# Batch 0's head: Q fetched by head halves, the first columns of w_in in four row chunks, one log and one scaling moved up, four fillers fewer

## The chip, the cores and the metric

The kernel runs on one core of a Trainium2 chip. The metric is device microseconds of that core; lower is better. A time covers a whole execution. The span, which the profile covers, is 1.7 to 1.9 us shorter in the runs of the kernel before: it runs from the first recorded instruction to the end of the last.

In the views, PE is TensorE's matmuls, PEld its weight loads, DVE is VectorE, ACT ScalarE, POOL GpSimd and SP SyncE; L674 is a line of the kernel. A landing is the moment at which the last byte of a transfer has arrived.

## The reference, cut to what matters

```python
def _attn_ref(q, k, v, g_norm):              # q, k, v: 8 batches, 8 heads, 576 rows, 64 columns
    kv = np.einsum('bhsd,bhse->bhde', k, v)
    out = np.einsum('bhsd,bhde->bhse', q, kv)
    rms = np.sqrt(np.mean(out * out, axis=-1, keepdims=True) + 1e-06)
    return out / rms * g_norm

def _moe_ref(x, w_in, w_out):                # 4608 x 512, 512 x 2048, 2048 x 512
    h = x @ w_in
    g = np.where(h > 0.0, h, np.exp(np.minimum(h, 0.0)) - 1.0)
    return g @ w_out
```

Linear attention without a softmax, a normalisation per head, then two dense products with an ELU between them. The two dense products are nearly all of the work, and TensorE (PE in the profile) does them.

## The kernel before: the parts that the change and the argument touch

Batch 0 has a head of its own. "Head" below means this first stretch of some 20 us, not an attention head. The order of the transfers (all on the GpSimd queue, except Q's two on SyncE's):

```python
fetch_q(0)                                   # two transfers of 512 KB: heads 0,2,4,6 then 1,3,5,7
packed_kv(0)
for c in range(4):                           # K and V of batch 0 in four pieces of 144 KB each
    fetch_packed_kv("k", 0, slice(c, c + 1))
    ...
    fetch_packed_kv("v", 0, slice(c, c + 1))
edges = (0, 512, 768, 1280, 1664, 2048)
for lo, hi in zip(edges, edges[1:]):         # w_in by columns, all 512 rows at a time
    load_w_in(slice(lo, hi))
load_w_out(0, 4)
fetch_packed_q(1)
load_w_out(4, 8)
packed_kv(1)
for name in "kv":
    fetch_packed_kv(name, 1, slice(0, 2))    # K and V of batch 1, first half
load_w_out(8, 10)
for name in "kv":
    fetch_packed_kv(name, 1, slice(2, 4))    # second half
```

The compute of the head goes by four chunks c of 128 rows of x transposed. Each is a K/V product, a score product, a square, a mean over the head's columns (a matmul with a matrix of 1/64), Ln, Exp with scale -0.5 (this is 1/rms), and a scaling on VectorE (DVE). Then come the first 24 products with w_in, six blocks of 128 columns, f, for four chunks, c. `idle(ps, n)` issues n filler matmuls on zeros.

```python
def square_first(c): nc.scalar.activation(sq0[c], se0[c], AF.Square)
def mean_first(c):   nc.tensor.matmul(mean0[c], lhsT=means, rhs=sq0[c], start=True, stop=True)
def log_first(c):    nc.scalar.activation(r0[c], mean0[c], AF.Ln, bias=eps_col)
def exp_first(c):    nc.scalar.activation(r0[c], r0[c], AF.Exp, scale=-0.5)
def scale_first(c):  nc.vector.scalar_tensor_tensor(out=x0[:, c, :], in0=se0[c], scalar=g_col,
                                                    in1=r0[c], op0=ALU.mult, op1=ALU.mult)
def first(fs, cs):
    for c in cs:
        for f in fs:
            nc.tensor.matmul(products[f], lhsT=w_in_sb[:, c, f * P : f * P + P],
                             rhs=x0[:, c, :], start=(c == 0), stop=(c == KC - 1))
...
se0[3] = bank(3)
se_first(3)
square_first(3)
exp_first(2)
idle(bank(0), 2)
scale_first(1)
scale_first(2)
...
first((0, 1, 2, 3), (0,))
mean0[3] = bank(2)
mean_first(3)
log_first(3)
exp_first(3)
scale_first(3)
products[5] = bank(1)
first((0, 1, 2, 3), (1, 2))
first((4,), (0, 1, 2))
first((0, 1, 2, 3), (3,))
first((5,), (0, 1, 2))
first((4, 5), (3,))
```

## Time and profile before

| | before |
|---|---|
| time, median of the first three runs | 284.17 us (284.15 to 284.39) |
| PE busy, share of the span | 98% |
| first product with w_in | 14.76 us |
| last Exp of the head starts | 16.77 us |
| next product stream after the head starts | 20.27 us |
| V of batch 1, second half: lands / the K/V product that needs it starts | 37.85 / 38.85 us |

The page's first part (busy microseconds, share of the span, instructions of each engine) and its fourth (the chain of work that ended last) of the kernel before:

```profile
PE 277.2 (98%) x2146; PEld 129.7 (46%) x2146; DVE 159.3 (56%) x231; ACT 154.5 (55%) x222; POOL 54.7 (19%) x96
...
PE 95%; DMA 2%; DVE 1%; SPq 0%; issue 0%; ACT 0%
```

PE is the bottleneck and waits for almost nothing. So only a stretch where PE has no useful work can give time, and that is the head.

The timeline of the kernel before, around the head and around batch 1. The columns are start, microseconds, engine, line, operation, output and inputs; brackets hold the idle time just before and what ended it:

```profile
14.76 0.33 PEld L674 LDWEIGHTS <-w_in_sb 128*128 128x128 bf16 x3 [0.39 <-DMA w_in_sb<-in_moe_w_in_dram]
14.76 0.60 PE L674 MATMUL h_ps<-xT,w_in_sb 128*128 128x512 bf16 x2
...
16.77 0.63 ACT L662 ACTIVATE r<-r 128x512 f32<-128x512 f32 x1
...
17.43 0.75 DVE L665 SCALAR_TENSOR_TENSOR xT<-bank,g_col,r 128x512 bf16<-128x512 f32 x1 [0.67 <-ACT r L662]
...
20.27 1.03 PE L465 MATMUL h_ps<-xT,w_in_sb 128*128 128x512 bf16 x4
...
38.85 0.48 PE L174 MATMUL at<-v_pk,k_pk 64*64 64x64 bf16 x36
```

The first product waits for w_in, which lands at 14.72. The K/V product at 38.85 has no bracket (one is printed for an idle time of 0.15 us and more): its V had landed a whole microsecond earlier.

```profile
q0 software_dynamic: 3334, 2.94, 90.9%
```

The transfers move about 205 GB/s from some 6 us to beyond 40 us without a pause. Apart from Q's two and the small g_norm, every transfer of the first 40 us stands in one line behind the others.

### The profile page before, as it was taken

Reading aid. Unit: us, or ns where it says so; the run is one execution under the profiler, and the core shown is the slowest. Engines: PE = TensorE matmul, PEld = TensorE weight load, DVE = VectorE, ACT = ScalarE, POOL = GpSimd, SP = SyncE. Lnnn points to the kernel's source line nnn. Section 1 sums busy time; section 2 is a strip of 40 time slices with the busy share of each in tenths; the row PEclk is TensorE's granted clock in tenths of the full one; section 3 lists DMA queues with packets and bytes.
Section 4 is the critical chain, followed back from the end, with each engine's and each line's share of the span. In section 5 each row is a group of like instructions: output and inputs, shape, how many; then the busy total and the mean of one; then the engine's idle time right before and its main releaser. Section 6 shows DMA issues by size and latency. Waiting matters only on the chain.

```text
span 282.7 us, 5187 instructions
## 1 busy us (share of the span) xinstructions
PE 277.2 (98%) x2146; PEld 129.7 (46%) x2146; DVE 159.3 (56%) x231; ACT 154.5 (55%) x222; POOL 54.7 (19%) x96
## 2 busy tenths in 40 slices
PE   7999999999999999999999999999999999999994
PEld 3444454445444444444444444444444444444443
DVE  2359443878388646944694468445854585444400
ACT  2779546667487438533863377237923792333311
POOL 7834422261421331005200421012000000000000
PEclk9999999999999999999999999999999999999999
DMA  7999999797993696358935794455233122010122
GB/s 194 203 204 202 208 200 185 220 152 129 187 190 62 154 166 148 74 148 124 196 75 145 93 216 84 116 115 150 55 97 73 78 53 95 0 77 0 74 74 77
DMA packets 56523, 35.99 MB, mean 127 GB/s; under 512 B 32820, under 2 KB 54068, under 8 KB 56500
## 3 DMA queue, kind: packets, MB, share of 16 engines
q0 software_dynamic: 20752, 17.30, 39.9%
q1 hardware_dynamic: 35348, 17.83, 23.7%
q10 hardware_dynamic: 400, 0.52, 0.6%
q8 instruction: 17, 0.28, 0.4%
q14 instruction: 6, 0.05, 0.0%
HBM read 36.70 MB, written 9.44 MB: 163 GB/s over the span
## 4 chain that ended last, share of the span: by engine, by line
PE 95%; DMA 2%; DVE 1%; SPq 0%; issue 0%; ACT 0%
PE h_ps L465 41%; PE o_ps L512 39%; PE o_ps L917 5%; DMA st_q<-in_q_dram 2%; PE at L174 2%; PE bank L674 1%; PE at L465 1%; PE at L201 1%; PE h_ps L674 1%; PE bank L596 1%; PE bank L644 1%; PE se_ps L201 1%; PE kv_ps L174 0%; PE at L185 0%; PE se_ps L413 0%; PE bank L656 0%
## 5 line engine op out<-in xcount | busy, mean ns | idle before, releaser
L465 PE MATMUL h_ps<-xT,w_in_sb 128*128 128x512 bf16 x536 | 125.7, 379 | 0.0
L512 PE MATMUL o_ps<-w_out_sb,gT 128*128 128x512 bf16 x512 | 120.5, 379 | 0.0
L477 ACT ACTIVATE elu_e<-h_ps 128x1024 bf16<-128x1024 f32 (+1 forms) x71 | 70.0, 995 | 79.9 <-PE h_ps L465 78.3
L465 PEld LDWEIGHTS <-w_in_sb 128*128 128x128 bf16 x552 | 52.5, 98 | 63.2 <-DVE xT L333 1.7
L512 PEld LDWEIGHTS <-gT 128*128 128x128 bf16 x512 | 49.4, 98 | 58.4
L488 DVE TENSOR_SCALAR elu_e<-elu_e 128x1024 bf16<-128x1024 bf16 (+1 forms) x75 | 32.3, 431 | 72.9 <-ACT elu_e L477 72.9
L496 DVE TENSOR_TENSOR gT<-elu_e,h_ps 128x1024 bf16<-128x1024 bf16 (+1 forms) x51 | 60.1, 1179 | 5.7 <-DVE elu_e L488 0.5
L525 ACT COPY o_sb<-o_ps 128x512 f32<-128x512 f32 x32 | 18.6, 586 | 15.6 <-PE o_ps L512 15.6
L218 DVE TENSOR_REDUCE ss<-sq 128x16 f32<-128x1024 bf16 x16 | 19.4, 1219 | 10.8 <-ACT sq L213 10.1
L483 ACT ACTIVATE elu_h<-h_ps 128x1024 bf16<-128x1024 f32 (+1 forms) x20 | 19.5, 990 | 0.0
L150 POOL COPY q_bf<-q_pk 128x512 bf16<-128x512 bf16 x24 | 14.6, 638 | 21.6 <-DMA q_pk<-in_q_dram 21.6
L496 DVE TENSOR_TENSOR gT<-elu_e,elu_h 128x1024 bf16<-128x1024 bf16 x20 | 13.8, 692 | 2.9 <-ACT elu_h L483 1.5
L917 PE MATMUL o_ps<-w_out_sb,gT 128*128 128x512 bf16 (+1 forms) x80 | 14.1, 337 | 0.0
L125 POOL COPY gate<-qT 1x1 bf16<-1x1 bf16 x6 | 1.1, 182 | 63.7 <-DMA qT<-q_bf 63.7
L104 POOL DMA_DIRECT2D q_pk<-in_q_dram x14 | 10.6, 762 | 2.8 <-issue 1.1
L229 DVE TENSOR_TENSOR xs<-at,ss 128x512 bf16<-128x512 f32 x16 | 10.3, 682 | 1.2 <-ACT ss L225 1.2
L917 PEld LDWEIGHTS <-gT 128*128 128x128 bf16 x80 | 7.7, 98 | 6.4 <-DVE gT L496 0.4
L213 ACT ACTIVATE sq<-at 128x1024 bf16<-128x1024 f32 x9 | 9.4, 1043 | 1.6 <-PE at L201 1.0
L118 POOL DMA_DIRECT2D k_pk<-in_k_dram x12 | 8.3, 691 | 4.5 <-DMA w_in_sb<-in_moe_w_in_dram 2.9
L596 PE MATMUL bank<-zeros 128*128 128x512 bf16 x20 | 7.8, 515 | 1.2 <-DVE zeros L573 1.2
L118 POOL DMA_DIRECT2D v_pk<-in_v_dram x12 | 8.2, 684 | 3.7 <-DMA w_out_sb<-in_moe_w_out_dram 1.8
L925 ACT COPY o_last<-o_ps 128x512 f32<-128x512 f32 (+1 forms) x5 | 2.5, 501 | 10.8 <-PE o_ps L917 10.8
(79 smaller groups left out, 139.4 us busy)
## 6 DMA issues: line engine op xcount, KB each, us to landing
out_dram<-o_sb SPq DMA_DIRECT2D x16, 512.0 KB, 3.0
q_pk<-in_q_dram POOLq DMA_DIRECT2D x14, 256.0 KB, 4.8
k_pk<-in_k_dram POOLq DMA_DIRECT2D x6, 576.0 KB, 8.3
v_pk<-in_v_dram POOLq DMA_DIRECT2D x6, 576.0 KB, 10.8
st_q<-in_q_dram SPq DMA_DIRECT2D x2, 512.0 KB, 5.1
w_in_sb<-in_moe_w_in_dram POOLq DMA_DIRECT2D x2, 512.0 KB, 8.8
w_out_sb<-in_moe_w_out_dram POOLq DMA_DIRECT2D x2, 512.0 KB, 15.2
w_out_sb<-in_moe_w_out_dram POOLq DMA_DIRECT2D x4, 256.0 KB, 11.8
```

Source lines behind the costliest of these rows:

```text
L118: nc.gpsimd.dma_start(out=raw[name, b].rearrange("p h j d -> p h (j d)")[:, hs], in_=in_[:, hs])
L150: eng.tensor_copy(out=out_, in_=in_)
L218: nc.vector.reduce_sum(out=ss, in_=sq.rearrange("p c (h e) -> p (c h) e", h=H), axis=AX.X)
L465: nc.tensor.matmul(h_ps[a][:, cs], lhsT=w_in_sb[:, c, f * P : f * P + P], rhs=x(c, cs), start=(c == 0), stop=(c == KC - 1),)
L477: nc.scalar.activation(e[:, lo:hi, :], ps, AF.Exp)
L483: nc.scalar.activation(h[:, lo:hi, :], ps, AF.Relu)
L488: nc.vector.tensor_scalar(out=e[:, lo:hi, :], in0=e[:, lo:hi, :], scalar1=1.0, scalar2=1.0, op0=ALU.min, op1=ALU.subtract,)
L496: nc.vector.tensor_tensor(out=gT[T][:, 2 * i + lo : 2 * i + hi, :], in0=e[:, lo:hi, :], in1=h, op=ALU.add if relu else ALU.max,)
L512: nc.tensor.matmul(o_ps[T, j], lhsT=gT[T][:, f, j * P : j * P + P], rhs=w_out_sb[:, f, :], start=(f == 0), stop=(f == FC - 1),)
L525: nc.scalar.copy(o_sb[T][:, j % 2, :], o_ps.pop((T, j)))
L596: nc.tensor.matmul(ps, lhsT=zeros[:, 0:P], rhs=zeros, start=True, stop=True)
L917: nc.tensor.matmul(ps, lhsT=gT[B][:, f, j * P : j * P + P], rhs=w_out_sb[:, f, cols], start=(f == 0), stop=(f == FC - 1),)
```

## The change

Its intent: w_in's first 512 columns should arrive by row chunks, so that the products of chunk 0 can start before all 512 KB are there. Q should come by head halves, so that the two head pairs that chunks 0 and 1 need arrive with the first transfer. Chunk 1's mean and log move ahead of chunk 2's score product and square, and chunk 0's scaling moves up, so that ScalarE's chain of Ln and Exp runs closer together. The 24 products are reordered, and net four filler matmuls go. Cut to its core:

```diff
-    fetch_q(0)
+    for u in range(2):                       # heads 0-3, then heads 4-7
+        nc.sync.dma_start(out=q_raw0[:, u]..., in_=q[0, 4 * u : 4 * u + 4, 0:G, :]...)
@@
-    edges = (0, 512, 768, 1280, 1664, 2048)
+    for c in range(KC):
+        load_w_in(slice(0, 512), slice(c, c + 1))
+        if c == 1:
+            load_w_in(slice(512, 768))
+    edges = (768, 1024, 1280, 1664, 2048)
@@
-    turn_first(qt_ps, (0, 1))
+    turn_first(qt_ps, (0, 2))
@@
     kv_first(0)
-    idle(idle_ps, 1)
+    turn_last(7, 1)
     se0[0] = bank(6)
     se_first(0)
     square_first(0)
@@
     log_first(0)
-    se0[1] = bank(7)
-    se_first(1)
-    square_first(1)
-    exp_first(0)
     g_ps = bank(1)
     nc.tensor.matmul(g_ps[:, 0:1], ...)      # g_norm, turned into a column
+    idle(idle_ps, 1)
+    se0[1] = bank(7)
+    se_first(1)
+    square_first(1)
+    exp_first(0)
@@
     kv_first(2)
-    idle(idle_ps, 2)
+    mean0[1] = bank(0)
+    mean_first(1)
+    log_first(1)
     se0[2] = bank(1)                         # then, as before, score product, square, exp_first(1)
     ...
+    scale_first(0)                           # taken out further down, with mean and log of chunk 1
@@
     se_first(3)
     square_first(3)
     exp_first(2)
-    idle(bank(0), 2)
     ...
-    first((0, 1, 2, 3), (1, 2))
-    first((4,), (0, 1, 2))
-    first((0, 1, 2, 3), (3,))
-    first((5,), (0, 1, 2))
-    first((4, 5), (3,))
+    first((0, 1, 2, 3), (1,))
+    first((4,), (0, 1))
+    first((0, 1, 2, 3, 4), (2, 3))
+    first((5,), range(KC))
```

The bytes moved are the same; there are four more transfers of w_in.

More of the change, by code (lines that the diff above doesn't have):

```diff
@@ L133, in unpack_q, with load_w_in @@
             copy_on(eng, bf["q", b][:, j], t[:, :, j])
-    def load_w_in(cols):
+    def load_w_in(cols, cs=slice(0, KC)):
         nc.gpsimd.dma_start(
-            out=w_in_sb[:, :, cols], in_=moe_w_in.rearrange("(c p) f -> p c f", p=P)[:, :, cols]
+            out=w_in_sb[:, cs, cols],
+            in_=moe_w_in.rearrange("(c p) f -> p c f", p=P)[:, cs, cols],
         )
@@ L549 @@
     V, A, Q = nc.vector, nc.scalar, nc.gpsimd
-    fetch_q(0)
-    q_raw0 = raw.pop(("q", 0))
+    q_raw0 = stage_tile("q")[:, 0:2048].rearrange("p (u x) -> p u x", u=2)
+    for u in range(2):
+        nc.sync.dma_start(
+            out=q_raw0[:, u].rearrange("p (h x) -> p h x", h=4),
+            in_=q[0, 4 * u : 4 * u + 4, 0:G, :].rearrange("h (p j) d -> p h (j d)", j=J),
+        )
     packed_kv(0)
@@ L603 @@
     idle(idle_ps, 9)
-    q_st = q_raw0.rearrange("p (q h j d) -> p q j h d", q=4, h=2, j=J)
+    q_st = q_raw0.rearrange("p u (l s j d) -> p u s j l d", l=2, s=2, j=J)
     q_two = attp.tile([P, NPAIR, J, 2, D], BF16, name="q_two", tag="q_two", bufs=1)
@@ L608, in cast_first @@
     def cast_first(pair, eng):
-        copy_on(eng, q_two[:, pair], q_st[:, pair])
+        copy_on(eng, q_two[:, pair], q_st[:, pair % 2, pair // 2])
     def turn_first(ps, pairs):
@@ L619 @@
     cast_first(0, V)
-    cast_first(1, A)
+    cast_first(2, A)
     qt_ps = turned(3)
-    turn_first(qt_ps, (0, 1))
-    nc.vector.tensor_copy(out=qT0[:, 0:2], in_=qt_ps)
+    turn_first(qt_ps, (0, 2))
+    nc.vector.tensor_copy(
+        out=qT0.rearrange("p (s u) t -> p u s t", u=2)[:, 0], in_=qt_ps
+    )
     idle(idle_ps, 4)
-    cast_first(2, V)
+    cast_first(1, V)
     cast_first(3, A)
@@ L680, in first, with turn_last @@
                 )
-    qt_ps = turned(7)
-    turn_first(qt_ps, (2,))
-    nc.scalar.copy(qT0[:, 2, :], qt_ps[:, 0, :])
+    def turn_last(n, pair):
+        qt_ps = turned(n)
+        turn_first(qt_ps, (pair,))
+        nc.vector.tensor_copy(out=qT0[:, pair, :], in_=qt_ps[:, 0, :])
     kv_first(0)
-    idle(idle_ps, 1)
+    turn_last(7, 1)
     se0[0] = bank(6)
@@ L689 @@
     square_first(0)
-    qt_ps = turned(0)
-    turn_first(qt_ps, (3,))
-    nc.vector.tensor_copy(out=qT0[:, 3, :], in_=qt_ps[:, 0, :])
-    idle_ps = bank(3)
+    turn_last(0, 3)
     kv_first(1)
@@ L709 @@
     )
+    idle_ps = bank(3)
+    idle(idle_ps, 1)
[3 more added lines that the diff above has]
+    exp_first(0)
     nc.vector.tensor_copy(out=g_col, in_=g_ps[:, 0:1])
+    idle(idle_ps, 1)
     kv_first(2)
-    idle(idle_ps, 2)
+    mean0[1] = bank(0)
+    mean_first(1)
+    log_first(1)
     se0[2] = bank(1)
@@ L715 @@
     square_first(2)
-    mean0[1] = bank(0)
-    mean_first(1)
-    log_first(1)
     exp_first(1)
+    scale_first(0)
     idle(idle_ps, 1)
     kv_first(3)
-    scale_first(0)
-    idle(idle_ps, 1)
     mean0[2] = bank(2)
@@ L734 @@
     pair = ps_head.tile([P, 2, G], FP32, name="h_ps", tag="kv")
-    products = {0: pair[:, 0, :], 1: pair[:, 1, :], 2: bank(6), 3: bank(7), 4: bank(0)}
+    products = {0: pair[:, 0, :], 1: pair[:, 1, :], 2: bank(6), 3: bank(0), 4: bank(7)}
     first((0, 1, 2, 3), (0,))
```

## The prediction

> **What bounds the kernel.** TensorE is busy 98% of the span (engine table) and the chain of waits is 95% PE. From 20.3 us on, the matmul starts show no gap over 0.31 us: 0.216 us per 512-column product, nothing else waited for. So only the head, before the first dense product stream, can give time. In the head: Q's two transfers land at 4.98 and 7.28 us (issue start plus time to landing), the K/V pieces one after another from 7.09 to 12.17, w_in's first 512 columns at 14.72. First product at 14.76, its weight load having waited 0.4 us for that transfer (waits). The head's 24 products plus one mean take 5.4 us at 0.216 each; the next product starts at 20.27: nearly dense from 14.8. So before is held by the landing of w_in's first piece, and just behind it by ScalarE: its last Exp ends at 17.40, the last scaling on VectorE at 18.18 (timeline).
>
> **What the change does.** The DMA queue is saturated here: 512 KB in 14.72-12.17 = 2.55 us, about 0.64 us per 128 KB row chunk. Estimated landings: rows 0 at 12.8, rows 1 at 13.5, columns 512-767 at 14.9, rows 2 and 3 at 15.5 and 16.1 (perhaps 1 us later: columns 512-767 took 2.3 us before, a straggler). Same bytes, four more transfers; their issues (0.55 to 0.75 us) stay ahead of the data. The weights no longer gate the first product.
>
> Head halves: pairs 0 and 2, all that chunks 0 and 1 need, come with the first Q transfer. Chunk 0's K/V product then waits only for V at 7.81 instead of running behind pair transposes at 8.11: start 7.87, first square 9.20 (was 9.44). A ScalarE copy (0.59) moves to VectorE. Net four filler matmuls (0.22 each) go.
>
> By the durations of before (square to Exp start 0.48, Exp to log 0.54, log to square 0.57, log to own Exp 0.72): logs at 10.26, 12.23, 13.86, 15.48; last Exp ends 16.83, last scaling 17.62. The last score product comes before the first product: first product about 14.1 (was 14.76). Then c=0 to 14.95, mean of chunk 3 about 15.06 (a small stall), c=1 from 15.3, c=2 from 16.6, c=3 from 17.68 just after the last scaling, f=5 last. Next product near 19.62 instead of 20.27: 0.65 us, all on the critical path.
>
> **Does it survive?** Later DMA landings stay where they are, bandwidth-bound: columns 768 on near 18.4 against use at 19.5; V of batch 1 (second half) lands 37.85, used at 38.85 before, so at 38.2 now. Slack about 0.4: a gain over 1.0 would be cut there. ScalarE, full from 20 to 28, starts its ELU work 0.8 us earlier too.
>
> **Prediction:** 283.5 us, range 283.1 to 284.0.
>
> **Right or wrong shows in:** first product near 14.1, not waiting for DMA; ScalarE's last head Exp ending near 16.8; the last scaling near 17.6; the first product after the head near 19.6; no new DMA wait on PE from 20 to 55; gap list after that unchanged.
>
> **What would make it wrong:** the small w_in pieces landing over 1 us late, moving the wait to columns 512-767 or rows 2 and 3; VectorE, in order, delaying a K/V copy behind a transposed-Q copy (0.42 each), so chunk 1's square starts late; [...] this trace shows fillers 0.43 us apart until 7.1 us and 0.22 after[...].

The gain is the 0.65 us from 20.27 to 19.62, off the 284.17 us before, so 283.5. Two statements have their figures in the traces: ScalarE was busy for 8.00 of the 8 us from 20 to 28 (before), and VectorE's order did cost chunk 1 a little (after: its K/V product ended at 10.06, its copy started at 10.15, behind a transposed-Q copy that ended at 10.12).

## More of the kernel before

The windows view of the kernel before (stretch, its length, busy time and instructions of PE, PEld, DVE, ACT and POOL, then the granted PE clock, the DMA share and the GB/s), and from the DMA view of its first 20 us the GpSimd queue's line (packets, MB, share):

```profile
11.00:13.00 2.00, 2.00 (x28) 0.87 (x28) 0.44 (x2) 1.63 (x4) 2.00 (x4) 1.00 1.23 205
...
16.00:20.00 4.00, 4.00 (x20) 1.76 (x18) 1.50 (x2) 2.36 (x4) 1.24 (x2) 1.00 1.29 204
```

## The result, and the profile after

| | before, same rounds | after |
|---|---|---|
| median | 284.21 us (284.15 to 284.39, 4 runs) | 284.54 us (284.26 to 285.21, 4 runs) |
| ratio after to before | | 1.0014, 95% interval 0.9996 to 1.0032 |

Ratios here are the mean time of one kernel's fast runs over the mean of the other's of the same rounds, so not quite the ratio of the medians. The result is "the same" at 2%, and no gain can be seen. The predicted 283.5 us was wrong, and so was its range: the median lies outside, above.

The same parts of the page after (source lines have moved: 465 is now 466, 174 is 175, 512 is 513, 674 is 685):

```profile
PE 274.2 (97%) x2111; PEld 130.0 (46%) x2142; DVE 159.8 (57%) x232; ACT 153.9 (54%) x221; POOL 56.7 (20%) x100
...
PE 84%; DMA 11%; POOL 2%; issue 1%; ACT 0%; POOLq 0%
```

PE's busy time fell (some matmul records are missing from a trace, so the 3 us are not to be taken at their word), but the span did not: both traced executions span 282.7 us. New in the chain is DMA, with 11%. The timeline after, at the same places:

```profile
8.08 0.47 PE L175 MATMUL kv_ps<-v_pk,k_pk 64*64 64x64 bf16 x18 [0.88 <-DMA v_pk<-in_v_dram]
...
10.95 0.40 PE L655 MATMUL bank<-qT,kv 64*64 64x512 bf16 x2 [0.25 <-DVE g_col L722]
...
14.33 0.61 PE L685 MATMUL h_ps<-xT,w_in_sb 128*128 128x512 bf16 x2
...
16.46 0.63 ACT L673 ACTIVATE r<-r 128x512 f32<-128x512 f32 x1
...
17.12 0.75 DVE L676 SCALAR_TENSOR_TENSOR xT<-bank,g_col,r 128x512 bf16<-128x512 f32 x1 [0.55 <-ACT r L673]
...
19.87 1.03 PE L466 MATMUL h_ps<-xT,w_in_sb 128*128 128x512 bf16 x4
...
38.68 0.48 PE L175 MATMUL at<-v_pk,k_pk 64*64 64x64 bf16 x36 [0.16 <-DMA v_pk<-in_v_dram]
```

The head did what it should. The first product no longer waits for w_in and starts at 14.33 instead of 14.76; the stream after the head starts at 19.87 instead of 20.27, 0.40 earlier. But at 38.68 there is a bracket that before did not have: the K/V product of batch 1 now waits for V. The chain of waits after shows the same, in order of time (start, microseconds, what):

```profile
14.20 11.90 DMA w_out_sb<-in_moe_w_out_dram
26.10 0.29 issue
26.39 12.15 DMA v_pk<-in_v_dram
38.54 0.14 issue
38.68 0.48 PE at L175 x36
```

V now lands at 26.39 + 12.15 = 38.54 us, 0.69 later than before's 37.85. The chain runs back through the queue: V's transfer is issued only when an earlier one has landed (w_out's at 26.10; GpSimd had waited 1.82 us for it, and as long in the kernel before, where V was issued at 25.92), so a delay of the early transfers is handed on. The same windows and the queue's line after:

```profile
11.00:13.00 2.00, 1.97 (x25) 0.81 (x25) 0.74 (x2) 1.72 (x4) 1.78 (x4) 1.00 1.20 179
...
16.00:20.00 4.00, 4.00 (x20) 1.83 (x19) 1.72 (x3) 2.50 (x5) 2.36 (x5) 1.00 1.39 198
```

```profile
q0 software_dynamic: 3769, 2.84, 93.5%
```

By 20 us the queue has moved 2.84 MB where it had moved 2.94, in more packets. 0.10 MB at 204 GB/s are 0.5 us: an estimate from these two traces that accounts for most of the 0.69. The other traces agree on the bytes: 2.94 to 2.96 MB in the four with before's transfers of w_in, 2.81 to 2.91 in the twelve with split ones.

To see what becomes of the 0.40 us, I matched each PE weight load after the head with the same one of the before trace, and took the difference of their start times. A step in this offset is a place where one kernel waits and the other does not.

| place in the before trace | 20.3 us | 39.5 | 58 | 90 | 277 | end of span |
|---|---|---|---|---|---|---|
| after minus before, us | -0.40 | -0.17 | -0.03 | +0.19 | +0.19 | -0.02 |

The largest steps are at V (0.23) and near 85 us (0.22). The second has its own cause. This is the timeline of DVE and POOL (GpSimd) at that place, before:

```profile
81.92 0.42 DVE L488 TENSOR_SCALAR elu_e<-elu_e 128x1024 bf16<-128x1024 bf16 x1
82.44 0.69 DVE L496 TENSOR_TENSOR gT<-elu_e,elu_h 128x1024 bf16<-128x1024 bf16 x1
```

and after:

```profile
81.89 0.85 DVE L489 TENSOR_SCALAR elu_e<-elu_e 128x1024 bf16<-128x1024 bf16 x1
82.85 0.91 DVE L497 TENSOR_TENSOR gT<-elu_e,elu_h 128x1024 bf16<-128x1024 bf16 x1
...
81.30 1.91 POOL L151 COPY q_bf<-q_pk 128x512 bf16<-128x512 bf16 x3 [3.56 <-DMA q_pk<-in_q_dram]
```

Two DVE operations took 0.85 and 0.91 us instead of 0.42 and 0.69 while POOL copied; before, the copies had ended at 80.61. Two other traces show the same: in e1, with copies from 80.57 to 82.48, the two took 0.57 and 0.91, and the next TENSOR_SCALAR, behind the copies, 0.41; in e6, with copies from 81.67 to 84.05, the three took 0.78, 0.91 and 0.83. Not every operation is longer beside a copy: the TENSOR_REDUCE at 78.87 in before took 1.22 with one, and 1.22 in after without. What makes the difference the traces do not show. In after the two longer operations make gT later, and PE's weight loads fall back by 0.22 just there (in e6, below, the wait for gT is in the view, 0.36 us). This is chance, not the change: of thirteen traces with the change or a part of it whose offset I followed, only this one and that of the fillers experiment (e6) have this step. Between 54 and 58 us another 0.14 went, which I did not trace to a cause. The last step, -0.21 between the end of PE's work and the end of the span, lies in the teardown behind the last store's landing. It is no chance: this stretch takes 1.19 to 1.21 us in the four traces of before's head (before, e2, e4, e16) and 0.97 to 0.99 in the twelve with the changed head. The four also have an 8 KB instruction fetch near the end (queue 14, one packet of 0.01 MB; the page of before has six with 0.05; at 283.0 in the before trace, 0.3 us past its span) and the twelve have none; whether that is the reason I did not test. So the changed head is worth 0.2 us here that the prediction did not have.

### The profile page after: what moved, and what is told of

It reads as the page before. It is cut to its first block, busy times and chain, and to the rows that moved or that the text cites. A ratio compares the mean times of both kernels' runs of the same rounds, so it can differ in the third digit from the quotient of the medians.

```text
span 282.7 us, 5151 instructions
## 1 busy us (share of the span) xinstructions
PE 274.2 (97%) x2111; PEld 130.0 (46%) x2142; DVE 159.8 (57%) x232; ACT 153.9 (54%) x221; POOL 56.7 (20%) x100
## 4 chain that ended last, share of the span: by engine, by line
PE 84%; DMA 11%; POOL 2%; issue 1%; ACT 0%; POOLq 0%
PE h_ps L466 39%; PE o_ps L513 36%; DMA v_pk<-in_v_dram 6%; PE o_ps L926 5%; DMA w_out_sb<-in_moe_w_out_dram 4%; POOL w_in_sb L136 2%; PE at L175 2%; PE at L202 1%; PE at L466 1%; PE se_ps L202 1%; PE se_ps L414 0%; POOL k_pk L118 0%; PE xt_ps L306 0%; PE at L306 0%; ACT o_last L934 0%
## 5 line engine op out<-in xcount | busy, mean ns | idle before, releaser
L513 PE MATMUL o_ps<-w_out_sb,gT 128*128 128x512 bf16 x488 | 118.1, 379 | 1.5 <-issue 0.5
L497 DVE TENSOR_TENSOR gT<-elu_e,elu_h 128x1024 bf16<-128x1024 bf16 x20 | 14.1, 703 | 2.5 <-ACT elu_h L484 1.0
L175 PEld LDWEIGHTS <-k_pk 64*64 64x64 bf16 x576 | 6.4, 107 | 5.5 <-issue 4.8
L934 ACT COPY o_last<-o_ps 128x512 f32<-128x512 f32 (+1 forms) x5 | 2.5, 501 | 10.8 <-PE o_ps L926 10.8
```

The lines of the kernel that those rows point to most:

```text
L175: nc.tensor.matmul(kv_ps[l * 64 : l * 64 + 64, s, u * 64 : u * 64 + 64], lhsT=bf["k", T][rows, j, 2 * u + l, :], rhs=bf["v", T][rows, j, 2 ...
L497: nc.vector.tensor_tensor(out=gT[T][:, 2 * i + lo : 2 * i + hi, :], in0=e[:, lo:hi, :], in1=h, op=ALU.add if relu else ALU.max,)
L513: nc.tensor.matmul(o_ps[T, j], lhsT=gT[T][:, f, j * P : j * P + P], rhs=w_out_sb[:, f, :], start=(f == 0), stop=(f == FC - 1),)
```

## The experiments

Four calls of several kernels each, on four different chips; each call shares its runs of the kernel before. Ratios compare within a call; offsets and landings are often compared across calls. All outputs were correct, but for e15, which is wrong.

### Is 284.5 reproducible, and which before trace is typical?

e1 is the changed kernel again, e2 the kernel before again, without an edit. e9, later, is the changed kernel.

> The changed kernel unaltered, to see which differences come back. Theory A (the head gains, a later DMA landing takes it back): head stream starts 0.3 to 0.5 us earlier than before (near 19.9 instead of 20.27), V of batch 1 second half lands near 38.5 instead of 37.85, TensorE waits for it at about 38.6, and the ratio lies in 0.999 to 1.001. Rival B (the trace of after was a chance run): V lands within 0.2 us of 37.85, no wait there, and the time is 0.3 us or more below before.

> The kernel before unaltered, as the null. All theories: ratio 1.000 within 0.0007, V landing near 37.85. If its own landing moves by over 0.3 us from run to run, theory A cannot be read from one trace.

> The changed kernel once more, for a trace. Three in ten of its executions had a span of 283.2 or more: if this is one, its trace shows either a late or withdrawn clock (matmuls 0.43 us apart after 7.5 us; theory K) or landings later than 38.8 with the clock whole (theory A). If it is a fast one: span near 282.1, like the run before.

Measured: e1 284.30 us (283.90 to 285.13, 6 runs), ratio 1.0011 (0.9997 to 1.0025). e2 284.20 (283.93 to 284.38, 5 runs), ratio 1.0002 (0.9990 to 1.0014). e9, one run, 285.1. The wait for V is there again in e1's timeline, although the whole execution runs 0.3 us earlier than the first one:

```profile
38.38 0.48 PE L175 MATMUL at<-v_pk,k_pk 64*64 64x64 bf16 x36 [0.17 <-DMA v_pk<-in_v_dram]
```

Two things follow. First, the before trace that I had predicted from was a late one: in e2, w_in's first piece landed at 14.49 instead of 14.72, and PE ran 0.29 us ahead of it all the way. Second, the runs of the changed kernel spread: of its 11 executions, four took 285.1 us or more, and seven lay between 283.9 and 284.7. The kernel before has no execution over 284.5 in 52. These slow ones are taken up below.

With all traces of before's head order (before, e2, and e16, which is told below and differs only by fillers) against all of after:

| offset to the first before trace, us | at 20.3 | at 39.5, behind V |
|---|---|---|
| before, e2, e16 | 0, -0.29, -0.43: mean -0.24 | 0, -0.29, -0.43: mean -0.24 |
| after, e1, e9 | -0.40, -0.71, -0.34: mean -0.48 | -0.17, -0.47, +0.03: mean -0.20 |

So by these means the head gains about 0.24 us, and after the K/V product of batch 1 nothing is left of it. Three traces of a kernel differ by 0.4 us, so both are rough: e1 against e2 alone has a gain of 0.42, of which 0.18 is left.

### Does the split of the transfers make V late?

e4 puts only the transfers of w_in on the kernel before; Q and all compute stay.

```diff
-    edges = (0, 512, 768, 1280, 1664, 2048)
+    for c in range(KC):
+        load_w_in(slice(0, 512), slice(c, c + 1))
+        if c == 1:
+            load_w_in(slice(512, 768))
+    edges = (768, 1024, 1280, 1664, 2048)
```

> Only w_in's transfers of the change, on the kernel before (row chunks of the first 512 columns, columns 512-767 after the second, columns 768-1279 in two). Theory A: the split itself costs about 0.5 us of landing, so V of batch 1 second half lands near 38.5, just ahead of its use at 38.8; the first product comes no later than 14.76, the time within 0.3 us of before. Rival C (the landing is later because Q's halves or the earlier products compete with the transfers): V lands near 37.85 here.

Measured: 284.42 us (284.34 to 284.99, 5 runs), ratio 1.0015 (1.0003 to 1.0027). V landed at 38.65. The windows view of e4:

```profile
11.00:13.00 2.00, 2.00 (x39) 0.88 (x40) 0.44 (x2) 1.62 (x4) 2.00 (x3) 1.00 1.17 168
```

168 GB/s where the kernel before has 205, and 2.83 MB by 20 us. The split alone makes the stall and makes V late; the compute is not needed for it.

e18 is the counterpart: the changed kernel with before's transfers of w_in and, for that, before's order of the 24 products. e17 is its base: the changed kernel with four fillers put back, which do no work but give PE's program before's length.

```diff
 e17:
+    idle(idle_ps, 2)                         # ahead of kv_first(0)
     kv_first(0)
     turn_last(7, 1)
+    idle(bank(2), 1)
     ...
     first((0, 1, 2, 3), (0,))
+    idle(bank(2), 1)
 e18, on top of e17: edges = (0, 512, 768, 1280, 1664, 2048) as before; products in before's order
```

> The changed kernel with four filler matmuls in TensorE's gaps of the head (two before chunk 0's K/V product, one before its scores, one before chunk 3's mean), nothing else: TensorE's program has the length of the kernel before. Theory F: no slow execution in six, last large instruction fetch near 275.5 to 276.5, last stores landing 1.7 and 2.2 us after issue, median 284.0 to 284.3. Rival (the split transfers make the slow executions): one to two of six still 0.8 us over.

> The same with w_in's transfers and the order of the 24 products as in the kernel before; Q by halves, the reordered chain and the four fillers stay. Theory A: no stall of the queue between 11 and 13 us, V of batch 1 second half lands near 37.9, TensorE does not wait for it, first product near 14.6 (gated by w_in), next stream near 20.1, so the total is within 0.2 us of before: without the split there is nothing to gain, with it the landing takes it back. Rival (the split costs nothing): slower than the run above by 0.3 us.

Measured: e17 284.08 us (283.99 to 285.05, 5 runs), ratio 1.0006 (0.9994 to 1.0019); e18 284.65 (284.44 to 284.73, 5 runs), ratio 1.0018 (1.0006 to 1.0031); the kernel before in that call 284.07. Timeline, windows and queue of e18:

```profile
14.89 0.60 PE L681 MATMUL h_ps<-xT,w_in_sb 128*128 128x512 bf16 x2 [0.49 <-DMA w_in_sb<-in_moe_w_in_dram]
```

```profile
11.00:13.00 2.00, 1.96 (x25) 0.81 (x25) 0.73 (x2) 1.72 (x4) 2.00 (x4) 1.00 1.24 206
```

```profile
q0 software_dynamic: 3358, 2.96, 92.0%
```

With whole pieces the stall is gone (206 GB/s, 2.96 MB by 20 us), V landed at 38.20, and nothing waited for it. But now the head waits 0.49 us for w_in, and its stream starts at 20.75 instead of e17's 20.08. So the split does in the head what it was meant to do for this order of compute, and costs V some 0.3 us (38.54 against 38.20; the changed kernel's own three traces spread as far as 38.24 to 38.74). The rest of V's lateness against before (38.20 against 37.85 to 37.94) is there without the split; in e18 the stretch from 5 to 8 us moved 211 GB/s against before's 227, and in after 201. The last V of batch 0, ahead of all of w_in, landed at 11.85 to 12.17 us in the four traces with before's Q (mean 11.98) and at 11.97 to 12.60 in the twelve with halves (mean 12.24), so Q by halves is the likely source. That was not tested alone.

### Can another cut of w_in have both?

e5 takes 768 columns by four row chunks, so fewer and larger pieces. e13 takes the rows in pairs.

```diff
 e5:
-        load_w_in(slice(0, 512), slice(c, c + 1))
-        if c == 1:
-            load_w_in(slice(512, 768))
-    edges = (768, 1024, 1280, 1664, 2048)
+        load_w_in(slice(0, 768), slice(c, c + 1))
+    edges = (768, 1280, 1664, 2048)
 e13, in place of after's whole loop and edges:
+    load_w_in(slice(0, 512), slice(0, 2))
+    load_w_in(slice(512, 768))
+    load_w_in(slice(0, 512), slice(2, 4))
+    edges = (768, 1280, 1664, 2048)
```

> The changed kernel with row chunks of 768 columns, and columns 768-1279 in one piece again (7 transfers, none of 256 columns). Theory A with the cause in the narrow packets (256 columns: 512 bytes): first product still near 14.3, V lands near 38.0, TensorE does not wait for it, 0.2 to 0.4 us faster than the changed kernel. Rival D (row chunks themselves read slowly, whatever their width): V lands near 38.4 still and nothing is gained.

> The changed kernel with w_in's first 512 columns in two transfers of two row chunks each instead of four of one, and columns 768-1279 whole. Theory S (a transfer of a single 128-row chunk is what makes the queue stall between 11 and 13 us): no stall, V of batch 1 second half lands near 38.0, TensorE does not wait for it. If the stall comes with the changed order or the head's timing: V lands at 38.3 or later, as in the changed kernel.

Measured: e5 284.15 us (283.92 to 286.6, 6 runs), ratio 1.0006 (0.9993 to 1.0019). e13 284.48 (284.31 to 285.18, 5 runs), ratio 1.0019 (1.0007 to 1.0031). In e13 V landed at 38.28, but the head waited for the second transfer in its middle:

```profile
17.44 0.60 PE L684 MATMUL h_ps<-xT,w_in_sb 128*128 128x512 bf16 x2 [0.80 <-DMA w_in_sb<-in_moe_w_in_dram]
```

e5's trace fell in its slow execution (286.6 us), so its head is no measure of the edit. Its transfers had 204 GB/s from 11 to 13 us, and V at 37.95; but e8, below, with the same transfers has 142 and 38.68, so this too may be peculiar to the slow execution. What made it slow is seen in its timeline and its windows (the third figure from the end is the granted clock):

```profile
8.28 0.47 PE L175 MATMUL kv_ps<-v_pk,k_pk 64*64 64x64 bf16 x18 [1.81 <-DMA v_pk<-in_v_dram]
```

```profile
11.00:13.00 2.00, 2.00 (x22) 0.76 (x21) 0.10 (x1) 1.27 (x3) 1.99 (x4) 0.50 1.17 204
13.00:16.00 3.00, 3.00 (x33) 1.12 (x27) 1.44 (x4) 1.85 (x4) 2.40 (x4) 0.50 1.19 210
```

PE idled 1.81 us for V, and from 10.8 to 17.6 us its clock was half: the record reads 0.50, and the two products at 16.47 took 1.04 us together where the two at 14.89 in e18 took 0.60. A matmul of 512 columns thus follows the one before it by about 0.43 us instead of 0.22. The fillers at the start have the longer spacing too, up to 7.06 us in before, 6.44 in after, 4.88 in e1 and 3.97 in e5, and the shorter one from there on. I read that as half and full clock, though the record of the granted clock reads 1.00 in before and after from the start. Before the drop in e5 PE was busy for 1.47 of the 3 us from 5 to 8 and for 2.67 of the 3 from 8 to 11; in after, whose clock stayed at 1.00 behind a gap of 0.88 us, it was 2.19 and 2.62, in before 2.69 and 2.86. The drop happened in this one of the traced executions; the other times of e5 show no such loss. That the gap caused it was not tested. The traces of after, e1 and e9 have the shorter spacing from 6.44 us on at the latest, so a slow clock is not the cause of after's usual time.

### Was it PE's idle time before chunk 0, or g_norm in the way?

The timeline after shows two flaws of the new order: PE idles 0.88 us at 8.08, and the score product of chunk 1 waits behind g_norm's product and its copy (10.95, where before had 10.54). e6 adds three fillers before chunk 0; e7 moves g_norm's product and copy ahead of chunk 0; e8 is e5's transfers with e7's g_norm and pair 1's transposes moved ahead as well.

```diff
 e6:
+    idle(idle_ps, 3)                         # ahead of kv_first(0)
 e7:
+    g_ps = bank(1); nc.tensor.matmul(g_ps[:, 0:1], ...); nc.vector.tensor_copy(out=g_col, ...)
     kv_first(0)                              # and the same lines taken out further down
 e8: e5 and e7, and
+    turn_last(7, 1)
     kv_first(0)
-    turn_last(7, 1)
```

> The changed kernel with three more filler matmuls just before chunk 0's K/V product, where TensorE waits for V at 7.2 to 8.1 us. Theory K (the slow executions of the changed kernel, spans of 283.1 and more, come from TensorE's clock being granted late or taken back after that gap, as in the 768-column run): no execution over a span of 283.0, spread under 0.6 us like before, median 0.2 us lower. Theory A alone (late transfers): the spread stays 1 us or more and the median stays near 284.3.

> The changed kernel with the g_norm product and its copy moved into that gap, so that chunk 1's scores are not behind it. All theories: the stream after the head starts 0.2 to 0.4 us earlier (near 19.4 to 19.6). Theory A: V of batch 1 second half still lands near 38.3 to 38.5, TensorE waits 0.4 to 0.6 us for it, and the total gains nothing (within 0.1 us of the changed kernel's fast executions). Rival: the gain reaches the end, 0.3 us.

> 768-column row chunks (as in the wide-rows run), the g_norm product and pair 1's transposes both moved before chunk 0's K/V product, so the gap is filled by useful work. Theory A and K together: V of batch 1 lands near 37.9, the stream after the head starts near 19.4[...], 283.6 us median, all executions within 0.5 us. If the slow executions stay, the transfers make them.

Measured: e6 284.25 us (283.71 to 284.77, 5 runs), ratio 1.0000 (0.9987 to 1.0013). e7 284.69 (283.92 to 285.17, 6 runs), ratio 1.0015 (1.0001 to 1.0030). e8 284.22 (283.87 to 284.59, 5 runs), ratio 1.0002 (0.9990 to 1.0014). e7 is the telling one. Its head is 0.18 us better than after's (stream at 19.69, offset -0.58), and at V all of the surplus goes: V lands at 38.61, PE starts at 38.74, the offset behind it is -0.10:

```profile
38.74 0.48 PE L175 MATMUL at<-v_pk,k_pk 64*64 64x64 bf16 x36 [0.41 <-DMA v_pk<-in_v_dram]
```

A better head is worth nothing past the landing of V. The other traces say the same. In nine of them (after, e1, e9, e4, e6, e7, e8, e12, e17) the product starts 0.14 us behind V's landing, and PE loses 0.02 to 0.48 us at this place; in all others V lands 0.20 us or more ahead of the product, and PE loses nothing there. In e8, with e5's transfers, V landed at 38.68 too, so that e5's landing at 37.95 is not owed to the cut alone. Theory K (the clock) does not explain the slow executions: e9's trace is one of them and has the full clock (matmuls 0.22 us apart) from 6.26 us on, and with the fillers of e6 the spread was still 1.06 us.

### Is it the queue's bytes ahead of V?

e15 leaves out 128 KB of w_out that are queued ahead of V and sets them to zero instead. Its output is wrong (relative error 0.2526). If V's landing is the limit, PE must pass it without a wait.

```diff
-    load_w_out(4, 8)
+    load_w_out(4, 7)
+    nc.gpsimd.memset(w_out_sb[:, 7, :], 0.0)
```

> The changed kernel with one 128 KB piece of w_out (rows 896 to 1023) not loaded but set to zero: wrong result on purpose, same work on TensorE, 0.64 us less of transfers ahead of V of batch 1. Theory A: V's second half lands near 37.8, TensorE's wait of 0.2 to 0.4 us at 38.7 vanishes, the offset to before that the head gains (0.4 to 0.5) lasts beyond 40 us, and the fast executions are 0.2 to 0.4 us faster than the changed kernel's (283.6 and less). Rival (the wait is not what takes the gain back): times as the changed kernel's, 283.9 to 284.3 for the fast ones.

Measured: 283.96 us (283.62 to 284.33, 5 runs), ratio 0.9996 (0.9983 to 1.0008). V landed at 38.23, and the timeline has no bracket:

```profile
38.43 0.48 PE L175 MATMUL at<-v_pk,k_pk 64*64 64x64 bf16 x36
```

The offset to the before trace is -0.41 at 20.3 us and still -0.41 at 277. This is the head's gain, kept to the end, in the one trace with a gain of this size whose V came ahead of its use. With e7, that the wait for V takes the gain is thereby shown. In time it made less than I expected: V came only 0.31 us earlier though the bytes left out stand for 0.6 at 205 GB/s (0.56 of it was still there when w_out's next piece landed, at 34.86 instead of 35.42; what took the rest is open), and the median is 0.13 below the kernel before of its call, inside the interval.

### Where do the slow executions come from?

e9's trace happens to be a slow execution (285.1 us, span 283.3). Its chain of waits ends, as the kernel before does, with the last copy on ScalarE (ACT), first before, then e9:

```profile
278.90 0.37 ACT o_last L925
```

```profile
278.92 0.37 ACT o_last L934
```

So up to there e9 stands level with the before trace, and its span's 0.6 us more lie behind it, in the last stores (0.8 us, less the 0.2 of the shorter teardown). The DMA view from 279.0 to 281.5 us (queue 8 carries instruction fetches: packets, MB, share; then the last stores with KB and microseconds to landing), before and then e9:

```profile
out_dram<-o_last SPq DMA_DIRECT2D x1, 64.0 KB, 1.9
out_dram<-o_last ACTq DMA_DIRECT2D x1, 64.0 KB, 2.2
```

```profile
q8 instruction: 1, 0.02, 3.1%
...
out_dram<-o_last SPq DMA_DIRECT2D x1, 64.0 KB, 2.9
out_dram<-o_last ACTq DMA_DIRECT2D x1, 64.0 KB, 3.0
```

A fetch of 16 KB of instructions (one packet of 0.02 MB; the page of before counts 17 on this queue with 0.28 MB) at 279.9 us fell on the last stores, and they landed 0.8 to 0.9 us later than they do without it. In the fourteen traces without a fetch at that place, the last two stores always took 1.9 and 2.2 us. The kernel before has this last fetch at 275.7, clear of the stores. e9's PE program is 8 rows shorter than before's, and that this had moved the fetch was the theory. Whose instructions queue 8 carries, no view says. e10 is the kernel before less four fillers, and nothing else; e16 is the same kernel again, for a trace, because e10's fell into an execution of 1016.72 us.

```diff
-    idle(idle_ps, 1)                         # behind kv_first(0)
-    idle(idle_ps, 2)                         # behind kv_first(2)
-    idle(bank(0), 2)
+    idle(bank(0), 1)
```

> The kernel before with four filler matmuls of the head taken away at places where TensorE waits anyway (one before chunk 0's scores, two before chunk 2's, one before the first product): TensorE's program is as long as the changed kernel's (8 rows less). Theory F (the slow executions come from TensorE's last 16 KB instruction fetch, which the shorter program moves from 275.5 us, before the last stores, to 280 us and later, onto them): head and V landing as before, but the last large fetch at 279 us or later or not in the record, and one to three of six executions 0.8 us or more over the rest; ratio about 1.001. Rival (only the transfers of w_in make slow executions): all executions within 284.5, ratio 1.000.

> The kernel before less four fillers again[...]. Theory F: the last large instruction fetch is not at 275.5 but at 279 us or later or outside the record; one or two of four executions 0.8 us or more over the rest, the others near 283.95. Rival: fetch at 275.5 as before.

Measured: e10 284.63 us median of 283.91, 283.98, 284.22, 285.03, 285.63 and one of 1016.72; ratio 1.0015 (0.9998 to 1.0033). The outlier is the execution that was traced: a 512-column matmul took 0.84 us in it, four times the usual, all the way through (from 500 to 600 us PE was busy for 98.29 us with 220 matmuls; the recorded granted clock nevertheless reads 1.00). It says nothing of the program. e16 284.52 (284.08 to 284.92, 4 runs), ratio 1.0013 (0.9998 to 1.0028). e16's trace shows the fetch again (chain of waits, then DMA view of the same window):

```profile
278.47 0.37 ACT o_last L923
```

```profile
q8 instruction: 1, 0.02, 2.4%
...
out_dram<-o_last SPq DMA_DIRECT2D x1, 64.0 KB, 2.6
out_dram<-o_last ACTq DMA_DIRECT2D x1, 64.0 KB, 2.8
```

Its PE ended 0.43 us ahead of the before trace, and its span is 0.1 us longer (282.8 against 282.7). Taking away four fillers that do no work made the kernel slower in the median in both, without any other change; each interval just reaches down to 1. The last traced fetch of each kernel sorts the same way: between 275 and 277 us in every trace of a program of before's length (before, e2, e4, e12, e17, e18) and in e6, two rows short of it; at 279.5, 279.9, 282 to 284 us, or not within the last 10 us at all, in the nine traces of programs 8 rows shorter (e10's, with its fourfold matmul times, not counted). Length alone does not fix the place: the changed kernel itself has it at 279.9, 283.0 and 283.3 in three traces.

Counting executions of 284.8 us and more (leaving out e10's 1016.72, with its matmuls of 0.84 us, and e5's 286.6, with its clock of 0.50 for 6.8 us): 13 of 46 for the programs 8 rows shorter, 2 of 25 for the changed kernels at or near before's length, none of 52 for the kernel before. Where the fetch meets the last stores, they land 2.6 to 3.0 us after issue instead of 1.9 and 2.2 (e9, e16).

Two points stay open here. Some slow executions (285.13 in e1, 285.63 in e10) have a normal span and 2.5 to 3.2 us outside of it, where executions of the kernel before have 1.7 to 1.9. Of the 48 executions of the shorter programs, 11 spent over 2.0 us outside; of the 25 at or near before's length none did, nor any of the kernel before whose span is on record. That these wait for the same fetch past the end is an inference, and two traces do not bear it out: after and e1 have the fetch 0.6 and 1.0 us past their spans' end, and only 1.8 and 1.9 us outside. And e4 and e17 had one slow execution each, at before's length, with a longer span; neither was traced.

### The best of both

e12 is e8 (e5's transfers, g_norm and pair 1's transposes early) with four fillers, for before's length.

```diff
 e8, and
+    idle(idle_ps, 2)                         # ahead of g_norm's product
     ...
     turn_last(7, 1)
+    qt_pad = bank(2)
     kv_first(0)
+    idle(qt_pad, 1)
     ...
     first((0, 1, 2, 3), (0,))
+    idle(bank(2), 1)
```

> 768-column row chunks, g_norm product and pair 1's transposes early, and four fillers in TensorE's gaps, so that its program is again as long as that of the kernel before. Theory F: last large fetch near 275.5 to 276.5, no execution more than 0.6 us over the fastest; median 283.9, at best 283.6 where V of batch 1 lands by 38.2. Rival: slow executions stay.

Measured: 284.06 us (283.94 to 284.19, 5 runs), ratio 0.9998 (0.9986 to 1.0010); the kernel before in that call 284.09 (283.93 to 284.32, 11 runs). No slow execution, the last fetch at 275.5, V at 38.45. It is the best complete version that I found, and it ties with the kernel before. Nothing that computes the right result beat both.

## Why the prediction was wrong, point by point

- "The weights no longer gate the first product": right. It starts at 14.33 with no DMA wait. Predicted were 14.1.
- The head chain: right in kind, 0.2 to 0.26 us late throughout. Chunk 0's K/V product started at 8.08 (V landed at 8.04, not 7.81; predicted 7.87), chunk 1's scores waited for g_norm's copy, the last Exp ended at 17.09 (16.46 + 0.63; predicted 16.83), the last scaling at 17.87 (predicted 17.62), the stream began at 19.87 (predicted 19.62).
- "0.65 us, all on the critical path": too large for two reasons. 0.25 is the lateness just named. And the 20.27 that it was taken from belongs to a late execution: other traces of before's head have 19.98 and 19.84. By the means above the head gained about 0.24 us.
- "Later DMA landings stay where they are, bandwidth-bound: ... V of batch 1 (second half) lands 37.85, used at 38.85 before, so at 38.2 now": this is the step that failed. I had costed the landings as bytes over a constant rate. The same bytes in smaller pieces, behind Q by halves, went slower: 179 GB/s instead of 205 from 11 to 13 us, 198 instead of 204 from 16 to 20. V landed at 38.54 (38.24 and 38.74 in the other two traces), and PE, which could have been there some 0.2 us earlier, waited. e4 shows that the split alone makes V late, e18 that whole pieces take the stall away, e7 that a better head gives no more, e15 that with V earlier the head's gain is kept.
- "Net four filler matmuls (0.22 each) go": counted as harmless or a gain. In the traces without them the last instruction fetch falls on the last stores (e9, e16), or past the end, or outside the record, and the kernel before without four of its fillers (e10, e16) became 0.13 to 0.15% slower by their ratios, whose intervals just include 1. This was in no term of the prediction.
- "A ScalarE copy (0.59) moves to VectorE", and Q by head halves: the transposes were no longer in the way, as predicted; the likely price was again DMA rate, 201 GB/s from 5 to 8 us instead of 227.
- The range of 283.1 to 284.0 assumed that one before trace and one mechanism were enough. The PE offset of one kernel varies by 0.3 to 0.4 us from trace to trace, half of the gain that I predicted.

Where the expected 0.65 went, then: 0.25 the head never gained, 0.16 was the late baseline (0.40 between the two first traces, 0.24 between the means of three), and the remaining 0.24 went at V's landing; the means are of few traces, so this split is rough. The 0.2 us of the teardown come on top as an unforeseen gain. That the median of after still exceeds before's by 0.15 to 0.33 is in e1 the slow executions: its quicker ones (283.90, 283.96, 284.12) lie where before's lie (283.92 to 284.47). It is not so in the four runs of the result: without 285.21 the other three, 284.26 to 284.63, are still above before's median of 284.21. The traced one of them (284.45) lost 0.36 us between 54 and 90 us that e1 and e9 did not lose; for the other two there is no trace. Open stays, too, why row chunks slow the queue down.

## What to carry to other kernels

A gain in one stage lasts only until the next wait that does not move with it (e7's 0.58 us were 0.10 behind V's landing): look for the next transfer whose landing sets a start, and ask whether the change moves that landing too, because splitting a load on a saturated queue was not free here, even at equal bytes (179 GB/s instead of 205 from 11 to 13 us). When a change is worth tenths of a percent, trace the unchanged kernel more than once and compare several executions before taking a gap in one trace as money. And if a program's length changes, by fillers too, look where the last instruction fetch falls: in e9 and e16 it fell on the last stores.

## What else the traces show of the hardware

- An instruction fetch of 16 KB on the last stores: these landed 2.6 to 3.0 us after issue instead of 1.9 to 2.2 (e9, e16), and in e16 only four fillers less had been needed.
- A granted clock of 0.50 for 6.8 us in one execution (e5), behind a gap of 1.81 us on PE and 2.5 us after it. Whether the gap caused it was not tested.
- Narrow pieces: with w_in's columns 768 to 1279 in pieces of 256 columns (512 B a row; after's queue moved 762 packets with 0.39 MB from 16 to 18 us) the queue moved 198 GB/s from 16 to 20 us, against 204 with 512 columns (1024 B a row). The last row chunk lies in the stretch too, but e8, e12 and e13 have row pieces there and columns 768 to 1279 whole, and moved 203 to 204. The eight usable traces with the narrow pieces moved 192 to 200.
- A load cut by rows on a busy queue: from 11 to 13 us the queue moved 138 to 181 GB/s where four row chunks came behind K and V (ten traces; e5, in its slow execution, 204) and 205 to 207 where one piece of 512 KB did (before, e2, e16, e18). The cause is open.
- In one execution (e10) matmuls of 512 columns took 0.84 us instead of about 0.21 for the whole 1015 us of the span, and the record of the granted clock read 1.00.
